# Gated mix of a long convolution and dilated local attention: transfers cut to multiples of 16 rows, the gate as a row, k and v all resident, late projections inside attention

## The chip, the cores and the metric

The kernel runs on one NeuronCore of a Trainium2 chip. TensorE (PE in the profile) multiplies matrices from SBUF into PSUM; VectorE (DVE) and ScalarE (ACT) move and change data between PSUM and SBUF; GpSimd (POOL) does small work and issues transfers; SyncE (SP) only issues transfers. All transfers, whoever issues them, run on 16 DMA engines. An engine works through its instructions in order, and so does the queue of a sequencer that issues transfers: an instruction that waits holds all behind it. The metric is the device time of one execution in microseconds.

## The reference

```python
g = sigmoid((x * gate_w).sum(-1, keepdims=True))      # x = A_q, [1, 2048, 640]
# branch a
k_shift = sum over t < 4 of shift_k[:, t] * k[s - t]  # causal, per channel
kv = k_shift * v
y = causal_convolution(kv, ssm_k) + kv * ssm_D        # by FFT over 4096 points
a = x * y
# branch b: 32 heads of 20 channels, window of 8 positions at a step of 2
q, k, v = split(x @ wqkv)
o = softmax(q[s] . k[s - 2 w] * 20 ** -0.5, w < 8, s - 2 w >= 0) @ v
b = o @ wo
out = g * a + (1 - g) * b
```

All inputs and the output are bf16.

## The kernel before

The program is written out by hand: instructions reach each engine in the order of the Python code, and a tile framework adds the waits. Memory is taken from pools; a pool that is closed leaves its room to later ones, whose first writers wait for the last users of what lay there. Of the transfers that SP issues, a new one waits for the one that was issued eight before it.

**Loading and v.** x is gathered into 18 tiles of 128 rows (`xS`): a tile holds two blocks of 64 keys, each with 57 queries and 7 rows before them, even and odd positions apart. `load_x` (L192) makes one transfer for blocks that are whole, and one of 57 or 62 rows where a sequence begins or ends. k is loaded as 16 consecutive positions in each partition, in four chunks of four, with a halo of three positions from the partition before (L216, 127 rows); v has two buffers (`vns`, L211), and chunks 2 and 3 are loaded from POOL's queue in `kv_gen` once a buffer is free. For each x tile PE makes five transposes (`transposes`, L280, evacuated by ACT to `xT`) and ten matmuls for v (`vproj`, L286, evacuated by ACT to `VW`).

**k*v** (`kv_gen`, L243) is DVE work: for each chunk four products with the taps (L248), two additions (L252, L255) and the product with v (L256) into a part of the same buffer `pr`, which POOL then writes to the scratch `kv_scr` (L260). It is advanced a step at a time between the PE work of the loops at L437 and L446.

**Gate** (`gate`, L301): 90 matmuls with one column each, exp, +1 and reciprocal, six transfers on POOL's queue that scatter the gate to `g_scr` in order of position (L314, L316), four that read it back (L318).

**q and k** (`qk_gen`, L331): five fifths (`ft`) of 128 channels; in each five groups of columns, k and q apart, five accumulating matmuls each (L340), evacuated (L342) to a staging tile `stg` with two buffers. When a fifth is done, SP sends its heads, 20 rows each, from `stg` to the attention's operand tiles `kq` (L355), where each head has 32 partitions: 20 channels and 11 feature rows that make the mask (`feats`, L323, eight loads of 374 KB). `kq[0]` lies where `xS` was, `kq[1]` where `kvw` (k and v) was; the latter's feature loads therefore wait for the last product of `kv_gen`.

**Attention**: 24 steps of four heads, in three groups `gi` of six x tiles each (eight steps `t` a group), each step in two halves. `scores` (L487) makes 24 small matmuls and one exponential into one of four `ET` buffers; `pv` (L501) makes 24 small matmuls into two PSUM tiles `O`, and after the second half DVE makes two reciprocals and two products. In the loop (L589) the scores of a half go ahead of the products of the half before. Beside it run `op_gen` (L573), the transposes and the output projection of the group before (one unit of work in a half, two in one of eight), and `ht_gen` (L469), 20 transposes on DVE of the filter `ssm_k`, which is loaded with its tap 0 corrected by `ssm_D` on POOL (`load_h`, L270). Results are stored to `b_scr` by two transfers of 57 rows per tile (`op_store`, L544). kv, G and wo are loaded as attention begins (L462 to L480).

**Convolution**: an FFT in matmul stages over five groups of 16 channels per quarter: `s1_gen` (L366) and `s2_gen` (L386) for the filter (h) and for kv (u); `h_s2` makes the copy `Hw` with its halves exchanged by two transfers (L406); `u_s2` multiplies spectra, four products on DVE after all four evacuations (L416, L417); `inv1` (L420) goes back. Evacuations go to ACT or DVE by a running estimate of their load (`Load`, L103). A last loop (L671) makes the last inverse stage, multiplies by the gated x (`qg`), adds the gated b (`bl`), and stores.

Of the kernel before, what the change touches and what calls it, by code (L numbers as in the profile page):

```python
# [131 lines left out]
def kernel(  # L132
# [33 lines left out]
    D5 = p0.tile([128, NG], BF, name="D5")  # L166
    gat = p0.tile([128, 18], F32, name="gat")
# [14 lines left out]
    wraw = pC.tile([128, D, 4], BF, name="wraw")  # L182
    wl = pC.tile([128, 4, D], BF, name="wl")
    pr = pC.tile([128, 4, 4 * D], BF, name="pr")
# [6 lines left out]

    def load_x(m0, m1):  # L192
        for sub in range(2):
            for m in range(m0, m1):
                k0, k1 = (PRE if sub == 0 and m % 9 == 0 else 0), (KB - 2 if sub == 1 and m % 9 == 8 else KB)
                if (k0, k1) != (0, KB):
                    nc.sync.dma_start(xs(m)[KB * sub + k0:KB * sub + k1],
                                      raw(x2, xrow(2 * m + sub, k0) * D, [[2 * D, k1 - k0], [1, D]]))
# [12 lines left out]
    vns = [kvw[:, (19 + 4 * e) * D:(23 + 4 * e) * D].rearrange("p (t d) -> p t d", d=D) for e in range(2)]  # L211

    def load_k(c):
# [3 lines left out]
        nc.sync.dma_start(kh[:, 3 + 4 * c:7 + 4 * c, :], raw(k2, 4 * c * D, [[16 * D, 128], [D, 4], [1, D]]))  # L217

    def load_v(c, eng):
        eng.dma_start(vns[c % 2], raw(v2, 4 * c * D, [[16 * D, 128], [D, 4], [1, D]]))  # L220
# [14 lines left out]
    for g in range(NG):  # L235
        nc.gpsimd.dma_start(D5[:, g:g + 1], raw(A_ssm_D, 16 * g, [[80, 8], [1, 16], [1, 1]]))
# [6 lines left out]
    def kv_gen():  # L243
        nc.vector.tensor_copy(wl[:], wraw[:].rearrange("p c j -> p j c"))
        yield
        for c in range(4):
            for j in (0, 1, 3, 2):
# [8 lines left out]
            nc.vector.tensor_tensor(pr[:, 2].rearrange("p (u n i) -> p n u i", u=8, n=4),  # L256
                                    pr[:, 0].rearrange("p (n u i) -> p n u i", n=4, u=8),
                                    vns[c % 2].rearrange("p n (u i) -> p n u i", u=8), ALU.mult)
            ld.t["d"] += 3000
            nc.gpsimd.dma_start(raw(kvs, 4 * c * 80, [[16 * 80, 128], [S * 80, 8], [1, 320]]),  # L260
                                pr[:, 2].rearrange("p (u m) -> p u m", u=8))
            if c < 2:
                load_v(c + 2, nc.gpsimd)
# [3 lines left out]

    hns = {}

    def load_h(g):  # L270
        hn = pA.tile([128, 2048], BF, name="hn", tag="hn", bufs=2)
        hns[g] = hn
        nc.sync.dma_start(hn[:], raw(A_ssm_k, IL * g * S, [[80 * S, 8], [S, IL], [1, S]]))
# [57 lines left out]
    def qk_gen():  # L331
        for ft in range(NDT):
# [13 lines left out]
            if ft == 0:  # L346
                feats(0)
# [374 lines left out]
```

## Time and profile before

| what | value |
|---|---|
| median of 2 runs | 417.5 us (417.04 to 417.96) |
| the profiled execution | 413.04 us, of which the span of the core is 410.6 us |
| mean granted TensorE clock of it | 0.728 |
| busy: PE, PEld (weight loads), DVE, ACT, POOL | 264.1, 190.4, 196.3, 175.2, 35.7 us |
| DMA | 48.95 MB in 15,152 packets, mean 119 GB/s |

The page cuts the span into 40 equal slices of 10.3 us; a digit is the busy share in tenths. The chain that ended last is followed back from the last instruction. A row such as "PE a L1 <- ACT b L2: 10, 3, 5" says that PE, at the instruction that writes a in line 1, waited three times for ACT, 10 us in all and 5 at most. A group's row gives the shapes, the count, busy us and mean ns, then the idle time before it. "issue" is time in which an engine waited for nothing that the profile shows.

### The profile page before, as it was taken

To read this page: it belongs to the slowest core of one execution; us is meant where nothing else is said; L and a number is where in the kernel's file an instruction comes from. 1 tells how busy PE (TensorE), PEld (TensorE's weight loads), DVE (VectorE), ACT (ScalarE), POOL (GpSimd) and SP (SyncE) were. 2 spreads that over 40 slices of the span, in tenths; PEclk is the share of its full clock that TensorE was granted. 3 is DMA by queue.
4 is the path that set the end of the run, shared out by engine and by line. 5 is a ranking of instruction groups with operands and counts; after the bars stand their busy time and mean duration, and the time that the engine had idled before them with its cause. 6 is when DMAs were issued, how large, how long until landed. Compare 5 with 4: busy or idle time off the path is not lost.

```text
span 410.6 us, 12313 instructions
## 1 busy us (share of the span) xinstructions
PE 264.1 (64%) x5611; PEld 190.4 (46%) x5616; DVE 196.3 (48%) x285; ACT 175.2 (43%) x292; POOL 35.7 (9%) x58
## 2 busy tenths in 40 slices
PE   1793099982965002773498999977644878678640
PEld 1572075540432000562365655655644867668530
DVE  0100689237015000392176833543752897966784
ACT  2483073513140002552243433432635696885372
POOL 6700011700110000000000000000000000000022
PEclk9998588996869555655555555799675798987875
DMA  7743877986523676469712010011599040429345
GB/s 205 158 125 103 271 276 114 110 174 90 136 72 62 86 128 129 99 165 211 282 51 81 18 32 24 28 42 58 124 213 245 17 105 4 105 54 232 80 106 155
DMA packets 15152, 48.95 MB, mean 119 GB/s; under 512 B 2639, under 2 KB 9661, under 8 KB 12700
## 3 DMA queue, kind: packets, MB, share of 16 engines
q1 hardware_dynamic: 12844, 42.11, 43.7%
q0 software_dynamic: 2256, 6.06, 6.7%
q8 instruction: 43, 0.70, 0.8%
q14 instruction: 9, 0.07, 0.1%
HBM read 29.43 MB, written 7.87 MB: 91 GB/s over the span
## 4 chain that ended last, share of the span: by engine, by line
DMA 27%; PE 26%; DVE 19%; issue 15%; POOL 5%; ACT 5%; SPq 1%; POOLq 0%; DVEq 0%; ACTq 0%
DMA kq<-stg 8%; DMA g_scr<-gat 6%; PE i L428 6%; PE op L553 6%; DMA Hw<-Hs 5%; PE O L521 3%; PE sc L496 3%; PE s L396 3%; DMA kv_scr<-pr 3%; DVE oS L531 2%; DVE hT L472 2%; DVE Hw L417 2%; DMA g_nat<-g_scr 2%; DMA b_scr<-fin 2%; PE tr L539 2%
## 5 line engine op out<-in xcount | busy, mean ns | idle before, releaser
L340 PE MATMUL pj<-xT,W 128*128 128x456 bf16 (+3 forms) x245 | 56.1, 395 | 47.5 <-ACT stg L119 47.2
L340 PEld LDWEIGHTS <-W 128*128 128x128 bf16 x250 | 27.0, 108 | 76.3 <-issue 57.8
L119 ACT CAST stg<-pj 128x512 bf16<-128x512 f32 (+3 forms) x50 | 24.9, 537 | 78.8 <-DMA kq<-stg 62.7
L499 ACT ACTIVATE ET<-sc 128x684 bf16<-128x684 f32 x48 | 35.4, 742 | 49.8 <-PE sc L496 48.5
L248 DVE TENSOR_TENSOR pr<-kvw,wl 128x2560 bf16<-128x2560 bf16 x16 | 23.1, 1483 | 68.8 <-DMA kv_scr<-pr 37.0
L472 DVE STREAM_TRANSPOSE hT<-hn 128x512 bf16<-128x512 bf16 x20 | 20.3, 1031 | 39.1 <-PE pj L340 39.1
L119 ACT CAST Am<-s 128x512 bf16<-128x512 f32 x59 | 31.2, 618 | 17.2 <-PE s L379 13.2
L428 PE MATMUL i<-M,Hs 128*128 128x128 bf16 x160 | 28.9, 269 | 9.1 <-DVE Hs L416 5.6
L553 PE MATMUL op<-wo,oT 128*128 128x320 bf16 x120 | 32.9, 432 | 2.8 <-DVE fin L558 2.6
L290 PE MATMUL psv<-W,xT 128*128 128x320 bf16 x180 | 30.3, 321 | 4.5 <-DMA W<-in_B_wqkv_dram 4.5
L428 PE MATMUL i<-M,Hw 128*128 128x128 bf16 x160 | 28.3, 268 | 4.3 <-DVE Hw L417 4.1
L396 PE MATMUL s<-Am,G 64*128 64x64 bf16 x1280 | 26.0, 203 | 7.6 <-DVE Am L121 3.9
L521 PE MATMUL O<-VW,ET 64*64 64x21 bf16 x1152 | 25.0, 203 | 8.9 <-issue 6.0
L496 PE MATMUL sc<-kq 31*64 31x57 bf16 x1152 | 25.0, 228 | 7.8 <-issue 6.1
L396 PEld LDWEIGHTS <-G 64*128 64x128 bf16 x1280 | 24.4, 104 | 9.1 <-issue 8.1
L496 PEld LDWEIGHTS <-kq 31*64 31x64 bf16 x1152 | 18.7, 141 | 19.6 <-issue 18.7
L428 PEld LDWEIGHTS <-Hw 128*128 128x128 bf16 x160 | 23.3, 156 | 8.4 <-DVE Hw L417 4.9
L428 PEld LDWEIGHTS <-Hs 128*128 128x128 bf16 x160 | 23.4, 157 | 7.4 <-DVE Hs L416 6.5
L521 PEld LDWEIGHTS <-ET 64*64 64x64 bf16 x1152 | 19.6, 142 | 12.7 <-issue 6.6
L529 DVE RECIPROCAL rd<-O 128x12 f32<-128x12 f32 x48 | 10.8, 224 | 28.5 <-PE O L521 28.2
L283 PE MATMUL trx<-ident,xS 128*128 128x128 bf16 x90 | 9.2, 244 | 23.2 <-DMA xS<-in_A_q_dram 23.2
L290 PEld LDWEIGHTS <-xT 128*128 128x128 bf16 x180 | 18.2, 105 | 11.6 <-issue 4.1
(65 smaller groups left out, 383.6 us busy)
## 6 DMA issues: line engine op xcount, KB each, us to landing
Hw<-Hs SPq DMA_DIRECT2D x10, 512.0 KB
kq<-stg SPq DMA_DIRECT2D x28, 170.2 KB
kq<-ca_feat SPq DMA_DIRECT2D x8, 374.3 KB
kvw<-in_A_k_dram SPq DMA_DIRECT2D x4, 640.0 KB
kv_scr<-pr POOLq DMA_DIRECT2D x4, 640.0 KB, 12.3
hn<-in_A_ssm_k_dram SPq DMA_DIRECT2D x5, 512.0 KB
kv<-kv_scr SPq DMA_DIRECT2D x4, 640.0 KB
qg<-in_A_q_dram SPq DMA_DIRECT2D x4, 640.0 KB
```

The source lines that it names most:

```text
L119: self.nc.scalar.copy(dst, src)
L248: nc.vector.tensor_tensor(pr[:, j].rearrange("p (n c) -> p n c", n=4), kh[:, 4 * c + 3 - j:4 * c + 7 - j, :], wl[:, j, :].unsqueeze(1).to_ ...
L290: nc.tensor.matmul(ps[:, 0:320], lhsT=xT[:, dt, 128 * m:128 * m + 128], rhs=W[:, dt, 2, n0:n0 + 320], start=(dt == 0), stop=(dt == NDT - 1))
L340: nc.tensor.matmul(ps[:, 0:nb * wd], lhsT=W[:, dt, which, 128 * ft:128 * ft + 128], rhs=rhs, start=(dt == 0), stop=(dt == NDT - 1))
L396: nc.tensor.matmul(o, lhsT=G[rows, j, r, :], rhs=Am[rows, 2 * j + r, :, :], start=(r == 0), stop=(r == 1), tile_position=(64 * c, 0), skip ...
L428: nc.tensor.matmul(o, lhsT=src[:, c, :, :, 8 * oc + il].rearrange("p q j -> p (q j)"), rhs=M[:, k, :], start=(k == 0), stop=(k == 1), skip ...
L472: nc.vector.transpose(hT[:, g].rearrange("p (c n) i -> p n c i", c=2)[:, 16 * p:16 * p + 16], hns[g][:].rearrange("p (a n) -> p n a", n=64 ...
L496: nc.tensor.matmul(sc[64 * sub:64 * sub + 64, hh, QB * mb:QB * mb + QB], lhsT=kqt[r:r + DH + NF, t % 4, si, 0:KB], rhs=kqt[r:r + DH + NF, ...
L499: nc.scalar.activation(ETs[i % NET][:, :, 0:NW], sc[:, :, 0:NW], ACT.Exp, scale=SCALE)
L521: nc.tensor.matmul(O_[s][64 * par:64 * par + 64, 21 * sl:21 * sl + 21], lhsT=ET[rows, hh, QB * mb:QB * mb + 64], rhs=VW[rows, NMB * gi + m ...
L529: nc.vector.reciprocal(rd[:], Ov[:, :, DH])
L553: nc.tensor.matmul(op[:, 0:320], lhsT=oTs[j][:, ft, :], rhs=wo[:, ft, 320 * hf:320 * hf + 320], start=(ft == 0), stop=(ft == NDT - 1))
```

## The change

Transfers. `load_x`, the halo and `op_store` are cut into a part with a multiple of 16 rows and a rest: 57 becomes 48 + 9, 62 becomes 48 + 14, 127 becomes 112 + 15. v has four buffers (`v23` is new), so that all of k and v is loaded on SP's queue, after all of x, and none on POOL's.

k*v. The product with v goes to its own tile `kvo` with two buffers; `kv_gen` is advanced from the first v tile on.

Gate. 30 matmuls with `wg` as the one stationary column give the gate as a row; six exps put it in order of position; SP writes it to `g_scr` in one transfer and reads it back in four; +1, reciprocal and 1 - g follow on DVE in `gate_end`.

Features. Only four transfers into the first of eight head slots; DVE copies the slot to the others, 14 copies.

q, k, v. k and q of a column group share one PSUM tile of two banks (three buffers), and likewise the two halves of a v tile, which ACT evacuates in one instruction. The last fifth of q/k and v tiles 12 to 17 are made inside the first attention group (`late_qk`, `late_v`), evacuated by DVE and ACT in turn.

Attention. The loop goes by whole steps: scores of the next step, then products, then late work, then two or three units of output projection. `O` is one PSUM tile of two banks with one buffer, with one reciprocal for both; the working PSUM tile `w` has two buffers instead of one.

Filter. No transposes: `load_h` makes eight transfers per group on POOL's queue, straight into the layout of the matmul (`h_lin`), in pieces of 64 elements; they, kv and G are issued when the first attention group is done. Tap 0 is corrected on DVE after attention.

Convolution. One evacuation for each s1 tile instead of two; the products with the spectra follow each of the four evacuations; the order of the s1 steps and the inverse steps changes.

```diff
+    def split16(n):
+        a = n - n % 16
+        return [(i, c) for i, c in ((0, a), (a, n - a)) if c]
...
-            nc.sync.dma_start(kh[1:128, 0:3, :], raw(k2, 13 * D, [[16 * D, 127], [D, 3], [1, D]]))
+            for p, n in ((1, 112), (113, 15)):
+                nc.sync.dma_start(kh[p:p + n, 0:3, :], raw(k2, (16 * p - 3) * D, [[16 * D, n], [D, 3], [1, D]]))
...
-    load_k(0); load_v(0, nc.sync)
     load_x(13, 18)
+    load_kv(0)
     load_w(1); load_w(0)
-    load_k(1); load_v(1, nc.sync); load_k(2); load_k(3)
+    for c in range(1, 4):
+        load_kv(c)
...
     def gate():
+        grow = pC.tile([1, S], F32, name="grow", tag="stg", bufs=2)
+        for c in range(6):
...
+                nc.tensor.matmul(gps[0:1, 0:6 * QB], lhsT=wg[:, dt:dt + 1], rhs=rhs,
...
+        nc.sync.dma_start(g_scr[:].unsqueeze(0), grow[:])
         for g in range(4):
+            nc.sync.dma_start(g_nat[32 * g:32 * g + 32, :], raw(g_scr[:], 16 * g, [[64, 32], [1, 16]]))
...
+        if e == 0:
+            nc.gpsimd.memset(kqt[:, 0], 0.0)
+            for h4 in range(4):
+                r = slice(32 * h4 + DH, 32 * h4 + DH + NF)
+                nc.sync.dma_start(kqt[r, 0].rearrange("p b c -> p (b c)"), ca["feat"].ap())
+    def feat_copies(e):
+        for t in range(4):
+            if e or t:
+                for p in range(2):
+                    ld.copy(kq[e][:, t, NSB * p:NSB * p + NSB], kq[0][:, 0, NSB * p:NSB * p + NSB], 800, eng="d")
...
+    def late_qk():
+        stg = new_stg()
+        for c in range(5):
+            for part in range(2):
+                ps = ppa.tile([128, 512], F32, name="pj2", tag="w", bufs=2)
+                qk_part(NDT - 1, c, part, ps)
+                qk_evac(stg, c, part, ps, eng="da"[part])
+                if (c, part) == (4, 1):
+                    qk_send(NDT - 1, stg)
+                yield
+    def late_v():
+        for m in range(12, 18):
+            for a in range(2):
+                ps = ppa.tile([128, 512], F32, name="pv2", tag="w", bufs=2)
+                vproj_half(m, a, ps[:, 0:320])
...
-    for m in range(18):
+    for m in range(12):
         vproj(m)
+        transposes(m + 2)
+        advance(kvg, 1)
+    for m in range(14, 18):
+        transposes(m)
     gate()
+    feats(0)
...
+    for k in range(20):
         advance(qk, 1)
         advance(kvg, 1)
+        if k >= 3:
+            advance(fc, 2)
+        if k == 12:
+            gate_end()
...
+    def load_h(g):
+        for q in range(4):
+            for c in range(2):
+                nc.gpsimd.dma_start(h_lin[32 * q:32 * q + 32, IL * g:IL * g + IL, c, :],
+                                  raw(A_ssm_k, (160 * q + 80 * c + IL * g) * S, [[64, 32], [S, IL], [1, 64]]))
...
+    for k in range(len(steps)):
+        if k + 1 < len(steps):
+            scores(2 * k + 2)
+            scores(2 * k + 3)
+        pv(2 * k)
+        pv(2 * k + 1)
+        gi, t = steps[k]
+        if gi == 0:
+            advance(lqk, (3, 3, 2, 2, 0, 0, 0, 0)[t])
+            advance(lv, (0, 0, 1, 2, 3, 3, 3, 0)[t])
+        if k == NT - 1:
+            sC.close()
...
+            load_h(0)
+            nc.sync.dma_start(G[:], cf["G"].ap().rearrange("p (a r b) -> p a r b", a=32, r=2))
...
+            for g in range(1, NG):
+                load_h(g)
         if opg is not None:
+            advance(opg, 3 if t % 2 else 2)
...
-        yield from s2_gen(("u", g), Up)
         Hs, Hw = st[("H", g)], st[("Hw", g)]
-        for c in range(2):
-            nc.vector.tensor_tensor(Hs[:, c], Up[:, c], Hs[:, c], ALU.mult)
-            nc.vector.tensor_tensor(Hw[:, c], Up[:, c], Hw[:, c], ALU.mult)
+        def prod(jb):
+            blk_ = lambda t_: t_[:, :, :, 8 * jb:8 * jb + 8, :].rearrange("p c q j l -> p (c q) (j l)")
+            for H_ in (Hs, Hw):
+                nc.vector.tensor_tensor(blk_(H_), blk_(Up), blk_(H_), ALU.mult)
+        yield from s2_gen(("u", g), Up, prod)
...
-                run("ababiabiabii", **gens)
+                run("ababababiiii", **gens)
```

More of the change, by code (lines that the diff above doesn't have):

```diff
@@ new lines, in qk_evac, with qk_send @@
+    def qk_evac(stg, c, part, ps, eng=None):
+        _, wd, _, z = QKP[part]
+        nb = 8 if c < 4 else 4
+        ld.copy(stg[:, 8 * c:8 * c + nb, z:z + wd], ps[:, 0:nb * wd].rearrange("p (b c) -> p b c", b=nb), nb * wd, eng=eng)
+    def qk_send(ft, stg):
+        for h in range(H):
+            r0, r1 = max(DH * h, 128 * ft), min(DH * h + DH, 128 * ft + 128)
+            if r0 < r1:
+                t, h4 = divmod(h, 4)
+                o = 32 * h4 + r0 - DH * h
+                nc.sync.dma_start(kq[t // 4][o:o + r1 - r0, t % 4, :, :], stg[r0 - 128 * ft:r1 - 128 * ft])
@@ L587 @@
     opg = None
+    lqk, lv = late_qk(), late_v()
+    steps = [(gi, t) for gi in range(NGI) for t in range(NT)]
     scores(0)
[L589 to L603 removed]
```

255 lines of the change are left out of this document (114 added, 141 removed).

## The prediction

> **What bounds the kernel now.** I read the page's parts 1, 2 and 4 first, then the waits, then the chain, then windows over the stages.
>
> ```profile
> span 410.6 us, 12313 instructions
> PE   1793099982965002773498999977644878678640
> DMA 27%; PE 26%; DVE 19%; issue 15%; POOL 5%; ACT 5%; SPq 1%; POOLq 0%; DVEq 0%; ACTq 0%
> ...
> PE trx L283 <- DMA xS<-in_A_q_dram: 23.2, 2, 16.2
> PE pj L340 <- ACT stg L119: 47.2, 3, 33.1
> ACT stg L119 <- DMA kq<-stg: 62.7, 3, 38.2
> DVE pr L248 <- DMA kv_scr<-pr: 37.0, 3, 20.9
> ```
>
> No engine is the bound as a whole: the largest share of the chain is DMA, and PE has holes in slices 4 to 16 (up to 167 us). The waits size them: one hole of 16.2 us in the transposes of x, and three holes, 47.2 us in all, where PE waits for ACT to empty a q/k accumulator, ACT itself waiting for the transfers out of `stg`.
>
> The first hole starts in SP's queue.
>
> ```profile
> 12.72 13.79 SPq L217 DMA_DIRECT2D kvw<-in_A_k_dram  x1
> ...
> 20.00:41.00 21.00, 14.14 (x128) 10.58 (x126) 0.00 (x0) 12.34 (x27) 0.00 (x0) 0.91 0.38 111
> 41.00:61.00 20.00, 10.67 (x80) 7.80 (x81) 15.80 (x10) 7.25 (x15) 1.46 (x2) 0.67 0.82 271
> ```
>
> In windows the last two columns are DMA share and GB/s. The load behind the 127-row halo of k holds SP for 13.79 us, and the DMA engines stand at 0.38 meanwhile: few of them do the work. The last x tiles queue behind it. After 41 us the same queue moves 271 GB/s.
>
> The other holes are one chain, here in order of time.
>
> ```profile
> 72.17 3.23 POOL g_scr L314 x2
> ...
> 79.10 26.59 DMA g_scr<-gat
> ...
> 116.91 4.23 DMA kv_scr<-pr
> ...
> 130.93 22.04 DMA kq<-stg
> 152.98 8.38 DMA kq<-stg
> ...
> kq<-ca_feat SPq DMA_DIRECT2D x8, 374.3 KB
> ```
>
> The gate's scatter (26.59 us) blocks POOL's queue, so the write of k*v chunk 2 leaves only at 116.91; DVE waits for `pr`, SP holds the second feature load until DVE is done, and the sends of the third fifth of q/k then share the engines with 4 x 374 KB of features (22.04 us), where the sends of a fifth alone take 8.38.
>
> ```profile
> 64.00:90.00 26.00, 25.84 (x131) 12.83 (x131) 11.94 (x9) 10.75 (x21) 8.93 (x8) 0.93 0.85 124
> 168.00:203.00 35.00, 18.14 (x841) 15.21 (x835) 16.45 (x40) 13.76 (x20) 0.26 (x4) 0.53 0.77 201
> 203.00:238.00 35.00, 32.31 (x769) 20.87 (x762) 24.38 (x51) 14.02 (x21) 0.57 (x3) 0.50 0.18 59
> 263.00:289.00 26.00, 19.86 (x392) 14.41 (x394) 11.99 (x28) 10.31 (x16) 0.00 (x0) 1.00 0.15 46
> ```
>
> Columns: window, length, busy time of PE, PEld, DVE, ACT, POOL, granted clock, DMA share, GB/s. Attention runs from about 167.5 to 289 us. Its middle third is PE-bound (32.31 of 35 us) at clock 0.50, though its end gets 1.00.
>
> **The change, part by part, as a new timetable.** The sum is made on the profiled span.
>
> *To the start of q/k (was 64 us).*
>
> ```profile
> 29.35 1.52 PE L290 MATMUL psv<-W,xT 128*128 128x320 bf16 x10
> L284 ACT COPY xT<-trx 128x640 bf16<-128x640 bf16 x18 | 12.4, 697 | 22.4 <-PE trx L283 22.2
> ...
> L305 PE MATMUL gps<-wg,xT 128*128 128x1 bf16 x90 | 2.4, 163 | 0.0
> ```
>
> Six of 18 v tiles leave: 6 x 1.52 = 9.1 us. The halo becomes 112 + 15 rows and goes behind all of x, so the 16.2 us hole goes; what is late next is nothing: 12 tiles last to about 32 us and x is some 4.4 MB with W and the filter, 16 us at 271 GB/s, 24 at two thirds of it. The gate becomes 30 matmuls of 342 columns, 0.16 us each by the row of 320 columns: 4.9 against 2.4 now, +2.5. Four trailing transposes go at ACT's 0.70 us: +1. So 64 - 9.1 - 16.2 + 2.5 + 1 = 42 us.
>
> *Four fifths of q/k (was 64 to 167.5).* 131 of 250 matmuls fill 26 us at clock 0.93, so a fifth is 9.9 us and four are 40: PE is done at 82. Sends keep pace (8.38 a fifth) with three accumulator pairs as slack. The features shrink from 8 loads of 374 KB to 4 of a quarter; the rest are 14 copies on DVE. The gate's 5 transfers move from POOL to SP: the sends now stand behind the landing of the gate's row, a few us, while the k*v writes stand behind nothing. The two PE holes before the third go; the third is replaced by DVE's k*v chain:
>
> ```profile
> L248 DVE TENSOR_TENSOR pr<-kvw,wl 128x2560 bf16<-128x2560 bf16 x16 | 23.1, 1483 | 68.8 <-DMA kv_scr<-pr 37.0 <-DMA kvw<-in_A_k_dram 31.7
> L252 DVE TENSOR_TENSOR pr<-pr 128x5120 bf16<-128x5120 bf16 x4 | 11.3, 2824 | 0.1
> L244 DVE COPY wl<-wraw 128x2560 bf16<-128x2560 bf16 x1 | 1.5, 1494 | 11.1 <-DMA wraw<-in_A_shift_k_dram 11.1
> kv_scr<-pr POOLq DMA_DIRECT2D x4, 640.0 KB, 12.3
> ```
>
> A chunk is 4 x 1.48 + 2.82 + two more of the first kind = 11.7 us, four are 47. Its first input lies 5.6 MB down the queue: 21 us at 271 GB/s, I take 25. Six feature copies come between, 2178 elements each: 1.27 us each by the copy row, 7.6 in all, and a wait of some 4 us for the features to land: 25 + 47 + 7.6 + 4 = 84. The first exponential's buffers lie where `kvo` lay, as far as the pools' order tells, so attention waits for the last k*v write: 4.2 to 12.3 us, I take 6. Attention starts at **90** (82 if PE alone counted, 97 at the upper prices). The Trainium skill, "VectorE: DVE Perf Modes", Rules for kernel authors, gives a dense bf16 copy in SBUF four elements a cycle, an estimate of 0.6 us each; then the six copies cost 3.8 and attention starts at 86. The only copy in the trace is strided, so no run here shows the dense one.
>
> *Attention, first group (was 167.5 to 203).*
>
> ```profile
> 225.15 0.65 PE tr L539 x5
> ...
> 226.70 1.45 PE op L553 x5
> 228.15 0.47 PE sc L496 x19
> 228.62 0.49 PE O L521 x21
> ...
> 264.19 0.84 PE L553 MATMUL op<-wo,oT 128*128 128x320 bf16 x5
> ...
> 264.96 0.38 PE L496 MATMUL sc<-kq 31*64 31x57 bf16 x24
> ```
>
> The upper rows are at clock 0.50, the lower at 1.00. A group's scores and products are 16 x 0.96 = 15.4 us slow, 12 fast (0.38 for each of the 32). The last fifth of q/k (9.9 fast, 19.8 slow) and a third of v (9.1, 18.2) come in. Fast: 31 us; slow: 53. These are long dense matmuls, like the 64 to 90 us window, so I take fast, with 6 us for a slow start and for the late sends, which the scores of t = 6 need: 37 us, to **127**. DVE's 20 transposes of h vanish, and its reciprocals halve in number; the single O buffer is covered by the late work and scores between two uses.
>
> *Second group (was 203 to 238).* The loads of kv and G move here from the first group, and with them its stalls:
>
> ```profile
> 191.07 0.48 PE L496 MATMUL sc<-kq 31*64 31x57 bf16 x18 [5.58 <-issue]
> 200.01 0.34 PE L521 MATMUL O<-VW,ET 64*64 64x21 bf16 x10 [5.96 <-issue]
> ```
>
> Both fall in the time when the queue moved 201 GB/s; PE waits for nothing that the profile shows. I take 9 of these 11.5 us, since the second group issues fewer instructions per us. Slow, the group is 12 x 1.45 + 6 x 0.65 + 15.4 = 36.7, which the 203 to 238 window confirms; fast it is 12 x 0.84 + 6 x 0.38 + 12 = 25 (a transpose taken as quick in proportion). Output projections now come two or three in a row instead of one between scores, so slow stretches should end sooner; I take 31 + 9 = 40, to **167**.
>
> *Third group and tail (was 238 to 289).* 25 fast, and for the last six tiles 6 x (2 x 0.84 + 0.38) = 12.4, 14 with waits for stores: 39, to **206**. Stores become 72 in place of 36, on an SP that has little else then.
>
> *Convolution (was 289 to 410.6, 122 us).*
>
> ```profile
> 298.02 19.11 DMA Hw<-Hs
> 349.78 1.23 DVE Hs L416
> ...
> 353.28 1.14 DVE Hw L417
> ```
>
> The copy Hw still queues behind 3.6 MB of qg and T (19.11). The four products (4.7 us, first and last of four rows shown) follow the last evacuation now; spread over it, about 1.3 stays. Over five groups they hold the chain for 12 us (if only the first two count) to 23.5; I take 15, so 9 are saved, less 3 because in the first group DVE now stops at its first product until Hw lands. Merged evacuations save perhaps 2. So 114, bounds 108 and 122. The additions of tap 0 are five tiny DVE operations.
>
> Sum: 90 + 37 + 40 + 39 + 114 = 320 span. The profiled execution took 413.04 for its span of 410.6, and the runs' median is 417.5, 1.1% above: 320 + 2.4 = 322, times 1.011 = **325**.
>
> **Rivals.** *Attention stays at half clock.* For it: 0.50 through 203 to 238 with PE 92% busy. Against: the denser blocks. It gives 53 + 46 + 37 + 15 = 151 in place of 116: 360 us.
>
> *The h loads gate the convolution, and the kernel gets slower.* The five loads of 512 KB become 40 on POOL's queue, 20,480 pieces of 128 bytes, from 127 us on; 79 us cover them, 3.9 ns a piece.
>
> ```profile
> L314 POOL DMA_DIRECT2D g_scr<-gat x4 | 6.4, 1596 | 0.6 <-DVE gat L309 0.6
> g_scr<-gat POOLq DMA_DIRECT2D x2, 2.0 KB, 26.0
> ```
>
> Issue alone at the L314 price (513 pieces) is 40 x 1.6 = 64 us, hidden. Landing: the k*v write moved 1,024 pieces in 4.23 us, 4.1 ns, 84 us in all: +5. The gate's 2,048 pieces of 4 bytes took from 72.2 to 105.7 us, 16.4 ns: 336 us in all, time 325 + 257 = 582. From about 8.4 ns a piece the kernel is slower than before. For the low price: the gate's scatter ran beside the sends of q/k in 57-row pieces. The Trainium skill, "DMA: Bandwidth & Descriptors", Specifications, asks for 512 bytes or more for line rate, which speaks against these loads; no run here shows 128-byte reads in bulk.
>
> *q/k stays transfer-bound*: sends of 20 rows are as before, and if the features or the gate's row land late each fifth costs 12 to 14 us instead of 9.9: 335 to 340. *The 16-row split does nothing*: then the 16.2 us hole stays in part, but halo after x leaves it to k alone: DVE's chain starts some 14 us later, 339.
>
> **How the numbers follow.** Main case 0.58 (300 to 345: attention from 82 to 97, groups fast or partly so, convolution 108 to 122); half clock throughout 0.20 (360); q/k or halo late 0.10 (335 to 345); h loads late but still a gain 0.07 (345 to 405); h loads slow enough to lose 0.05. Range 300 to 360, the likeliest alone 305 to 342. Two per cent is about what a measurement of this kernel can tell from no change: faster 0.93, same 0.02, slower 0.05.
>
> **What would show it.** Right: no wait of PE for x beyond 13 us; PE's waits for `stg` under 5 us; first exponential near 90, released by the last `kv_scr` write; clock near 1.0 in the first group; two stalls of about 5 us in the second; h landed before the last projections. Wrong: PE idle in the convolution's first stage until `h_lin` lands, clock 0.5 through attention, or ACT waiting for `kq<-stg` by tens of us.

## The result, and the profile after

The changed kernel takes 335.24 us (median of two runs, 332.93 and 337.55) where the kernel before takes 417.5: a ratio of 0.803, 95% interval 0.779 to 0.827. The forecast was 325 in a range of 300 to 360. Beside the runs further down the kernel before had medians of 404.6 to 414.1 us, so its 417.5 is on the long side and the ratio lies nearer 0.81 to 0.83. A run more than 1.5% above the fastest of its kernel counts as slow, and medians in this document are those of the other runs, while ranges take in all. The profiled execution took 337.55 us for a span of 335.7, so against the span of 320 in the forecast's sum 15.7 us are missing.

The page of the changed kernel, its span, PE's busy share and clock in 40 slices of 8.4 us, the instruction queue's share of DMA, and the chain by engine:

```profile
span 335.7 us, 12259 instructions
...
PE   1399899969549978643969987536696969677330
...
PEclk9999999999757997555877999567778797985855
...
q8 instruction: 43, 0.70, 0.9%
...
PE 35%; DVE 22%; DMA 13%; issue 12%; ACT 10%; SPq 5%; POOL 0%; DVEq 0%; ACTq 0%; POOLq 0%
```

From slice 3 to slice 10 (84 us), where the kernel before had its holes, PE is nearly full, and DMA has gone from 27% of the chain to 13%. The low digits are elsewhere: slices 11 and 12 (84 to 101 us), 17 to 19 (134 to 159) and most of what follows 208 us.

The same execution by stage: window, length, busy time of PE, PEld, DVE, ACT, POOL, granted clock, DMA share, GB/s. The last four rows are the three groups of attention, cut at the first exponential of each, and the convolution up to its first inverse matmul.

```profile
0.00:43.80 43.80, 29.95 (x240) 21.18 (x242) 16.85 (x11) 22.95 (x37) 16.27 (x22) 1.00 0.97 283
43.80:83.70 39.90, 37.06 (x200) 19.20 (x206) 31.72 (x24) 18.55 (x39) 2.85 (x3) 1.00 0.51 119
```

```profile
86.50:128.80 42.30, 33.23 (x827) 19.93 (x829) 19.05 (x43) 16.12 (x27) 2.05 (x5) 0.76 0.46 103
128.80:169.30 40.50, 26.28 (x870) 18.45 (x857) 13.06 (x34) 15.00 (x24) 24.53 (x39) 0.62 0.83 192
169.30:193.00 23.70, 20.20 (x810) 15.00 (x803) 12.28 (x33) 14.17 (x21) 1.24 (x2) 0.86 0.19 51
208.90:243.70 34.80, 18.86 (x544) 17.06 (x545) 19.95 (x24) 19.29 (x20) 0.00 (x0) 0.67 0.74 173
```

The same points in the two traces, the groups in both by their first exponentials:

| reached (us of the span) | before | forecast | after |
|---|---|---|---|
| start of q/k | 64 | 42 | 43.8 |
| PE done with the q/k made ahead | 167.6 | 82 | 83.7 |
| first exponential | 169.1 | 90 | 86.5 |
| start of the second group | 193.5 | 127 | 128.8 |
| start of the third group | 235.4 | 167 | 169.3 |
| start of the convolution | 286.9 | 206 | 208.9 |
| length of the convolution | 123.7 | 114 | 126.8 |

Up to the convolution the timetable held within 4 us at every point. The convolution was to gain 8 us and lost 3; with 126.8 in place of 114 it is 13 of the missing 15.7. Of the span 74.9 us are gained in all, and the table says where: 82.6 lie ahead of the first exponential. Attention takes 122.4 us where it took 117.8, now with a fifth of q/k and a third of v inside it, and the convolution 3.1 more.

What PE waits for now, first in the waits (total, times, longest), then in the timeline (start, length, the idle time before it in brackets):

```profile
PE s L445 <- issue: 11.6, 5, 6.7
PE sc L539 <- issue: 8.9, 3, 5.4
PE pj L349 <- ACT stg L119: 7.7, 2, 5.0
PE O L561 <- issue: 4.9, 1, 4.9
```

```profile
98.50 2.29 PE L349 MATMUL pj<-xT,W 128*128 128x512 bf16 x5 [5.00 <-ACT stg L119]
...
135.98 0.55 PE L539 MATMUL sc<-kq 31*64 31x57 bf16 x26 [1.69 <-issue]
146.56 0.33 PE L539 MATMUL sc<-kq 31*64 31x57 bf16 x9 [5.43 <-issue]
155.50 0.66 PE L561 MATMUL O<-VW,ET 64*64 64x21 bf16 x35 [4.90 <-issue]
172.82 0.37 PE L539 MATMUL sc<-kq 31*64 31x57 bf16 x10 [1.76 <-issue]
223.36 0.88 PE L445 MATMUL s<-Am,G 64*128 64x64 bf16 x26 [6.73 <-issue]
```

The three holes of 47.2 us in q/k are down to 7.7. The largest sum is now "issue", time in which PE waited for nothing that the profile shows: 12.0 us in the second group (1.69, 5.43 and 4.90), 1.76 at the start of the third, 6.73 in the first stage of the convolution. Those of the second group and of the convolution fall where DMA is full (shares 0.83 and 0.74).

### The profile page after: what moved, and what is told of

The parts are those of the page before. It is cut to its first block, busy times and chain, and to the rows that moved or that the text cites. A ratio compares the mean times of both kernels' runs of the same rounds, so it can differ in the third digit from the quotient of the medians.

```text
span 335.7 us, 12259 instructions
## 1 busy us (share of the span) xinstructions
PE 238.3 (71%) x5549; PEld 175.0 (52%) x5556; DVE 188.4 (56%) x279; ACT 168.8 (50%) x247; POOL 52.9 (16%) x81
## 4 chain that ended last, share of the span: by engine, by line
PE 35%; DVE 22%; DMA 13%; issue 12%; ACT 10%; SPq 5%; POOL 0%; DVEq 0%; ACTq 0%; POOLq 0%
PE i L482 8%; PE op L595 6%; DVE pr L256 6%; PE s L445 5%; DMA kq<-stg 5%; ACT Am L119 4%; PE O L561 3%; DVE pr L260 3%; PE sc L539 3%; DMA xS<-in_A_q_dram 3%; PE pj L349 3%; DMA kvw<-in_A_k_dram 3%; DVE kq L121 3%; SPq L363 2%; ACT Up L119 2%
## 5 line engine op out<-in xcount | busy, mean ns | idle before, releaser
L119 ACT CAST stg<-pj 128x456 bf16<-128x456 f32 (+3 forms) x45 | 21.4, 531 | 35.0 <-PE pj L349 17.7
L445 PE MATMUL s<-Am,G 64*128 64x64 bf16 x1280 | 25.6, 201 | 15.9 <-issue 11.6
L631 POOL DMA_DIRECT2D h_lin<-in_A_ssm_k_dram x40 | 25.8, 650 | 56.0 <-PE sc L539 40.3
L445 PEld LDWEIGHTS <-G 64*128 64x128 bf16 x1280 | 23.7, 103 | 17.4 <-issue 15.6
L119 ACT CAST Am<-s 128x1024 bf16<-128x1024 f32 x25 | 24.1, 1060 | 12.8 <-PE s L430 8.4
L755 POOL DMA_DIRECT2D out_dram<-qg x12 | 6.0, 502 | 154.6 <-DVE qg L753 154.6
L595 PE MATMUL op<-wo,oT 128*128 128x320 bf16 x120 | 25.4, 359 | 3.8 <-ACT oT L582 2.3
L539 PE MATMUL sc<-kq 31*64 31x57 bf16 x1152 | 16.9, 206 | 14.6 <-issue 8.9
L568 DVE RECIPROCAL rd<-O 128x24 f32<-128x24 f32 x24 | 7.4, 306 | 34.5 <-PE O L561 34.5
L287 PE MATMUL psv<-W,xT 128*128 128x320 bf16 x120 | 20.8, 326 | 5.1 <-DMA W<-in_B_wqkv_dram 5.1
L119 ACT CAST Cm<-i 128x1024 bf16<-128x1024 f32 x13 | 13.1, 1012 | 19.7 <-PE i L482 19.7
L582 ACT COPY oT<-tr 128x640 bf16<-128x640 bf16 x18 | 12.5, 692 | 20.0 <-PE tr L579 19.7
```

The source lines that it names most:

```text
L119: self.nc.scalar.copy(dst, src)
L287: nc.tensor.matmul(ps, lhsT=xT[:, dt, 128 * m:128 * m + 128], rhs=W[:, dt, 2, 320 * a:320 * a + 320], start=(dt == 0), stop=(dt == NDT - 1))
L445: nc.tensor.matmul(o, lhsT=G[rows, j, r, :], rhs=Am[rows, 2 * j + r, :, :], start=(r == 0), stop=(r == 1), tile_position=(64 * c, 0), skip ...
L539: nc.tensor.matmul(sc[64 * sub:64 * sub + 64, hh, QB * mb:QB * mb + QB], lhsT=kqt[r:r + DH + NF, t % 4, si, 0:KB], rhs=kqt[r:r + DH + NF, ...
L582: nc.scalar.copy(oT[:], tr[:])
L595: nc.tensor.matmul(op[:, 0:320], lhsT=oTs[j][:, ft, :], rhs=wo[:, ft, 320 * hf:320 * hf + 320], start=(ft == 0), stop=(ft == NDT - 1))
```

## The experiments

All edits are made to the changed kernel. Where two runs are compared, the lengths of stages from their traces are used beside the times. The times of one kernel spread over 1 to 3%, so 2 or 3 us can't be read from them alone.

### The parts that made the gain: rows of 16, and the gate

```diff
-        return [(i, c) for i, c in ((0, a), (a, n - a)) if c]
+        return [(0, n)]
...
-            for p, n in ((1, 112), (113, 15)):
+            for p, n in ((1, 127),):
```

The loads of x and the stores to `b_scr` go whole here as well.

> The changed kernel with the multiples of 16 rows taken back: loads of x with 57 or 62 rows, the halo of k with 127 rows and the stores to b_scr with 57 rows go whole again; the places in the queues stay as they are. Theory G (the split is what counts; the forecast's rival gave 339 us for a split without effect): the halo holds SP for about 14 us, DVE's k*v chain ends about 14 us later, the stores of the tail land in 3.6 to 3.9 us instead of 1.4, in all 12 to 25 us slower. Rival H (the place behind x did it alone): within 4 us.

Measured: 360.78 us (359.69 to 361.48), ratio 0.8815 (0.875 to 0.888). Three rows of its timeline and the window of the first, then the same window of the changed kernel:

```profile
19.42 13.67 SPq L225 DMA_DIRECT2D kvw<-in_A_k_dram  x1
...
50.34 5.70 DVE L256 TENSOR_TENSOR pr<-kvw,wl 128x2560 bf16<-128x2560 bf16 x4 [36.72 <-DMA kvw<-in_A_k_dram]
...
54.49 27.15 PE L349 MATMUL pj<-xT,W 128*128 128x512 bf16 x127 [11.59 <-DMA W<-in_B_wqkv_dram]
```

```profile
19.40:33.10 13.70, 13.70 (x127) 10.49 (x125) 0.00 (x0) 10.90 (x18) 0.00 (x0) 1.00 0.25 59
```

```profile
19.40:33.10 13.70, 13.70 (x129) 10.57 (x128) 4.79 (x4) 10.75 (x17) 0.00 (x0) 1.00 1.06 300
```

PE does the same work in both windows, but DMA moves 59 GB/s in place of 300, because SP stands behind the halo of 127 rows. With the halo behind x, what comes late is W for q/k (11.6 us of PE) and the first input of the k*v chain: its first product starts at 50.34 us and not at 28.30. So the chain is 22 us late, where theory G had 14; the first exponential comes at 107.3, 20.8 us later, and from the last exponential to the convolution, where the stores lie, it takes 2.9 us more. Theory G holds, at the top of its 12 to 25. The Trainium skill, "DMA: Bandwidth & Descriptors", Why a DMA increments its semaphore by 16 and not by 1, says that a transfer is spread over the largest number of engines up to 16 that divides the slowest dimension on both sides, and names 127 partitions as a case with one engine. The trace's list of DMA packets agrees: the 127 packets of the halo, 3,840 bytes each, go one behind the other there, from 26.6 to 48.2 us and never more than two at once; in the changed kernel up to 16 of them run at once, from 21.0 to 25.9 us.

For the gate its old functions were put back: 90 one-column matmuls, six scatters and four loads on POOL.

```diff
-        nc.sync.dma_start(g_scr[:].unsqueeze(0), grow[:])
...
+                nc.gpsimd.dma_start(raw(gs, 2 * QB * sub + e, [[2, QB], [4 * QB, n], [1, 1]]),
+                                    gat[KB * sub + PRE:KB * sub + KB, 9 * e:9 * e + n].unsqueeze(2))
...
+            nc.gpsimd.dma_start(g_nat[32 * g:32 * g + 32, :], raw(gs, 16 * g, [[64, 32], [1, 16]]))
```

> The changed kernel with the old gate: 90 matmuls of one column, and six scatter transfers and four loads on POOL's queue in front of the writes of k*v, with the second buffer of kvo kept. Theory I (the gate on POOL's queue was the cause of the third hole): the write of chunk 1 or 2 leaves only when the scatter has landed, some 26 to 34 us after the gate; DVE stands at kvo, the k*v chain ends 8 to 15 us after 86.4 and the time grows by as much, less 2.5 us of PE. Rival J (two kvo buffers hide it): within 3 us.

Measured: 357.94 us (357.67 to 361.29), ratio 0.8766 (0.868 to 0.885), 22 us above the changed kernel's 336.05 in the control run below. From its timeline:

```profile
63.53 2.04 POOL L321 DMA_DIRECT2D g_nat<-g_scr  x4 [6.12 <-DMA g_scr<-gat]
...
67.42 3.73 POOL L333 MEMSET kq<- 128x4356 bf16 x1 [0.15 <-issue]
...
78.62 1.37 DVE L121 COPY kq<-kq 128x2178 bf16<-128x2178 bf16 x2 [21.78 <-DMA kq<-ca_feat]
...
92.32 2.93 PE L353 MATMUL pj<-xT,W 128*128 128x512 bf16 x7 [22.71 <-ACT stg L119]
```

POOL's queue is the cause, as the forecast said, but what stands behind the scatter is not a write of k*v: it is the memset of the feature slot. The features land late, DVE waits 21.78 us for them at a copy, the k*v chain behind the copy waits with it, and PE stops for 22.71. Theory I had the place right, the victim and the size (8 to 15) wrong.

These two parts are 25 and 22 us of the gain. That features now come in four loads and copies instead of eight loads, and that k, v and `kvo` have more buffers, was taken back in no run; what these are worth is not known.

### Late projections inside attention

```diff
-        for ft in range(NDT - 1):
+        for ft in range(NDT):
...
-    for m in range(12):
+    for m in range(18):
...
-            advance(lqk, (3, 3, 2, 2, 0, 0, 0, 0)[t])
-            advance(lv, (0, 0, 1, 2, 3, 3, 3, 0)[t])
```

> The changed kernel with all q/k and v products made before attention again (18 v tiles, five fifths), nothing late inside the first group. In the control on its chip the first exponential came at 86.6 us and the first one of the second group at 128.0. Theory K (moving the products only filled a wait; their 19 us of PE work are the same at either place): the first exponential comes at 102 to 105 us, since the last fifth now covers the wait for the third fifth's sends, the first group takes 15 to 18 us in place of 41.4, the second group begins at 118 to 122, and the time falls by 5 to 9 us. Rival L (the long matmuls inside the first group keep the clock high and cover the waits of scores, exponentials and products for each other): without them the first group has a clock near 0.5 and takes 22 to 28 us, the second begins at 126 to 131, and the time is within 3 us of the changed kernel or up to 3 us longer.

Measured: 342.0 us (338.91 to 343.34), ratio 0.8298 (0.822 to 0.838), which still touches the interval of the changed kernel. First exponential at 105.8, near theory K's 102 to 105, but the first group then took 39.1 us:

```profile
105.80:144.90 39.10, 12.78 (x744) 10.83 (x743) 6.70 (x20) 11.14 (x18) 11.64 (x18) 0.56 0.93 196
```

```profile
112.92 0.81 SPq L656 DMA_DIRECT2D G<-cf_G  x1
...
122.29 0.71 PE L538 MATMUL sc<-kq 31*64 31x57 bf16 x47 [5.43 <-issue]
133.38 0.43 PE L538 MATMUL sc<-kq 31*64 31x57 bf16 x16 [8.72 <-issue]
143.69 0.62 PE L560 MATMUL O<-VW,ET 64*64 64x21 bf16 x32 [7.56 <-issue]
149.62 0.72 PE L538 MATMUL sc<-kq 31*64 31x57 bf16 x48 [3.32 <-issue]
```

PE is busy 12.78 of 39.1 us. The clock of 0.56 is what L expected, but the time goes to three stalls, 21.7 us in all (5.43, 8.72 and 7.56; the last row's 3.32 lies in the second group). xT and W give up their room earlier, so G, kv and h are loaded from 112.9 us on, straight into a group that has only small matmuls. Both theories fail on the main point: K had 15 to 18 us for the group, L 22 to 28. By these rows the late work buys, above all, that the loads start behind the first group.

### What the stalls without a cause are

In one experiment G and kv alone were issued one by one, each behind a store of the second group; in the other h as well, over the second and the third:

```diff
+            if pending:
+                nc.sync.dma_start(*pending.pop(0))
```

> The changed kernel with the five loads of G and kv not issued at once behind the first attention group but one at a time (G in two halves), each behind a store of a finished tile in the second group. Theory B (big loads in a row starve PE of its instructions, because each 16 KB packet of the instruction queue stands behind them): the stalls without a named cause in the second group, 13.8 us in all (1.7, 5.4, 4.9 and 1.8), shrink below 4 us, and the time falls by 8 to 12 us. Rival D (the 40 loads of h in pieces of 128 bytes cause them, or the program itself): the stalls stay within 3 us of 13.8 and the time within 3 us. If G or kv land too late, PE waits for them in the convolution's first stage.

```diff
+            pending += [0, gl(0), 1, gl(1), 2, kl(0), kl(1), 3, kl(2), kl(3), 4]
...
+                    nc.gpsimd.tensor_copy(tick[:], fins[j][0:1, 0:1])
+                    load_h(nxt)
```

> The changed kernel with the loads of h, G and kv issued one group at a time (0.5 to 1 MB each), each behind a store of a finished tile in the second and third attention groups: the eight transfers of an h group wait on POOL for one element of the tile just finished. Theory B' (whatever keeps the engines full holds up PE's instructions, the h pieces among it, since spreading kv and G alone left 10.6 of 13.8 us): stalls without a named cause under 4 us in the second group, which ends some 10 us earlier, and 8 to 12 us off the time. Rival M (the program stalls there whatever is loaded, or the paced loads stall PE in the third group instead): within 3 us of the changed kernel beside it.

> The changed kernel as it is, as the control on this chip for the runs beside it and for the ones before: 331 to 337 us, ratio 0.80 to 0.82; its convolution, 127.2 us in the first profile and 123.7 to 128.5 in the five runs that left its code alone, again within 123 and 129.

| kernel | median us (range) | second group | third group | start of convolution |
|---|---|---|---|---|
| changed | 335.24 (332.93 to 337.55) | 40.5 | 23.7 | 208.9 |
| changed again, f0 | 336.05 (335.14 to 338.60) | 41.1 | 24.3 | 211.4 |
| d1, G and kv spread | 335.77 (332.94 to 338.07) | 33.9 | 28.4 | 207.4 |
| f1, h too | 330.94 (329.35 to 338.13) | 30.5 | 30.4 | 206.8 |

```profile
128.40:158.90 30.50, 24.60 (x868) 17.47 (x858) 13.35 (x35) 14.79 (x24) 13.13 (x23) 0.72 0.36 98
158.90:189.30 30.40, 22.73 (x806) 16.42 (x800) 12.09 (x32) 14.27 (x22) 8.99 (x17) 0.72 0.73 162
```

These are the second and third group of f1. With the DMA share of the second down from 0.83 to 0.36, the group loses 10 us, as B' said; the third, which now gets the loads (0.73 in place of 0.19), takes 6 to 7 us more, as M said. Of the stalls over 1 us, the second group keeps 4.2 us of 12.0 and the third has 6.1 in place of 1.8. So each theory is right about one of the groups: a good part of the cost goes where the loads go. The two groups together take 60.9 us instead of 64.2 (65.4 in f0). The median is 5 us below f0's, but the ranges overlap, and over all runs it is 2; neither the 8 to 12 of B' nor M's limit of 3 is shown by the times. d1 lies between: stalls of 1.2, 3.0 and 3.8 us in its second group and of 3.8 in its third, the second 6.6 us shorter, the third 4.7 longer, the time unchanged. Its theory B had the time wrong, its rival D the second group.

The mechanism shows in the trace's list of DMA packets. The queue "q8 instruction" moved 43 packets, 16 KB each. Each long stall ends a short and nearly equal time after such a packet began:

```
changed kernel: packet begins  133.44 144.00 152.72 169.96 220.59 231.37
                PE goes on     135.98 146.56 155.50 172.82 223.36 234.12
f2:             packet begins  119.89 130.63 140.96 146.75
                PE goes on     122.29 133.38 143.69 149.62
```

That is 2.4 to 2.9 us in ten of ten. In all fourteen traces 103 waits of PE over 1.5 us have no named cause; each ends 2.2 to 3.5 us after a packet began. And PE goes on at even steps of its program: counted in all the instructions of PE in the trace (matmuls, weight loads, semaphore waits), the ends of the first three long stalls of the changed kernel lie 256 apart, and from one of the 103 to the next of the same trace it is always a multiple of 256, to within 2. So PE goes on when its next piece of program has come, and the piece waits behind the loads. That the stalls follow the loads was shown by f1 and f2; how the two queues share an engine was not. Loads are not the only ground: in the last loop of the convolution, whose matmuls are short (148 in 1.48 us), the changed kernel has a stall of 2.27 us while the DMA share is 0.02.

### The hole at 92 to 98 us

```diff
-            advance(lqk, (3, 3, 2, 2, 0, 0, 0, 0)[t])
-            advance(lv, (0, 0, 1, 2, 3, 3, 3, 0)[t])
+            advance(lqk, (0, 3, 4, 3, 0, 0, 0, 0)[t])
+            advance(lv, (4, 1, 0, 0, 2, 3, 2, 0)[t])
```

> The changed kernel with the late v products first and the last fifth of q/k a step later (calls per step 0,3,4,3 and 4,1,0,0,2,3,2 in place of 3,3,2,2 and 0,0,1,2,3,3,3). Theory E (PE stands from 92.4 to 98.5 us because the staging tile of the last fifth waits for the sends of the third, and other work is at hand): the hole shrinks to under 2 us and the time falls by 4 to 6 us. Rival F (the last sends come later by as much, and the scores of t = 6 wait for them): the hole moves to t = 6 or 7, time within 2 us.

Measured: 335.13 us (334.1 to 337.08). The hole of 5.0 us is down to 1.81 and 0.63:

```profile
93.65 2.82 PE L287 MATMUL pv<-W,xT 128*128 128x320 bf16 x10 [1.81 <-DVE VW L121]
...
114.78 0.38 PE L539 MATMUL sc<-kq 31*64 31x57 bf16 x23 [1.17 <-DMA kq<-stg]
117.43 0.38 PE L539 MATMUL sc<-kq 31*64 31x57 bf16 x23 [1.14 <-DMA kq<-stg]
123.69 0.38 PE L539 MATMUL sc<-kq 31*64 31x57 bf16 x23 [1.41 <-DMA kq<-stg]
```

Short waits for the last sends come in its place (3.7 us in these three, 4.6 with one of 0.92; the changed kernel has 1.9), and the second group begins at 127.9 instead of 128.8: theory F.

### The convolution

```diff
-        yield from s2_gen(("u", g), Up, prod)
+        yield from s2_gen(("u", g), Up)
+        for c in range(2):
+            nc.vector.tensor_tensor(Hs[:, c], Up[:, c], Hs[:, c], ALU.mult)
+            nc.vector.tensor_tensor(Hw[:, c], Up[:, c], Hw[:, c], ALU.mult)
```

> The changed kernel, with one part of its convolution put back: the spectral products follow all four evacuations of a group (four instructions of 2048 elements in place of eight of 1024 spread over the evacuations). The convolution took 127.2 us where the forecast had 114. Theory A (the new order costs): the first products stand in DVE's queue until Hw lands, so undoing them brings the first inverse matmul nearer to the landing and the time falls by 3 to 6 us. Theory B (the loads of qg and T cost: PE stands 6.7 us without a named cause and Hw lands 24.8 us after the start of the stage): no change, within 2 us. Theory C (the forecast's own term: spread products save 9 us, and the loss lies elsewhere): slower by 6 to 12 us.

```diff
-                run("ababababiiii", **gens)
+                run("ababiabiabii", **gens)
...
-                run("bbbbiiii", **gens)
+                run("bbibibii", **gens)
```

> The changed kernel, with the old order of first-stage and inverse steps in the convolution (two first-stage steps, then an inverse step, and so on, in place of all eight first-stage steps ahead of the four inverse ones). Theory A: the inverse matmuls no longer wait behind the merged evacuations on ACT, which the chain shows in rows of 4.7 and 4.8 us in two groups: faster by 4 to 8 us. Theory B: within 2 us. Theory C: the spread products need the evacuations to come first, because the inverse stage waits for the last product: slower by 2 to 6 us.

The third has both, and `ld.copy` of 512 elements twice in place of 1024 once in `s1_gen`:

> The changed kernel with all three edits of the convolution put back (products last, old interleave, two evacuations for each first-stage tile); the filter stays as it is loaded now. Theory A: the convolution comes to 114 to 119 us, the time falls by 8 to 13. Theory B: within 3 us of the changed kernel, the stall of 6 to 7 us in the first stage and the landing of Hw some 25 us after its start stay. Theory C: slower by 9 us or more, 136 us of convolution.

In the fourth the loads of qg and T stand behind `run("abababab", a=h_s2(0), ...)` instead of ahead of it:

> The changed kernel with the five loads of qg and T issued behind the first Hw transfers instead of ahead of them. Theory B: PE's stall of 6.7 us in the first stage goes or shrinks below 2, Hw lands 10 to 14 us after the start of the convolution instead of 24.8, and the time falls by 8 to 12 us. Theory A: Hw lands earlier, but what follows (evacuations on ACT, products on DVE) was the limit anyway: faster by at most 3 us. If the stall stays while no load of qg is under way, neither is right about it and it belongs to the program itself.

| kernel | median us (range) | convolution | to the first inverse matmul | the rest |
|---|---|---|---|---|
| changed | 335.24 (332.93 to 337.55) | 126.8 | 34.8 | 92.0 |
| changed again, f0 | 336.05 (335.14 to 338.60) | 125.4 | 35.6 | 89.8 |
| c1 products last | 331.38 (330.12 to 333.35) | 120.2 | 31.4 | 88.8 |
| c2 old interleave | 330.69 (328.99 to 333.48) | 119.0 | 29.7 | 89.3 |
| c3 all three old | 334.40 (332.08 to 337.43) | 126.3 | 29.7 | 96.5 |
| c4 qg, T later | 331.69 (331.02 to 340.27) | 126.7 | 31.3 | 95.4 |

The ratios of c1 to c4 (0.802, 0.800, 0.808, 0.804) are too near each other for the times to decide. The stage is clearer: in the eight profiles that leave it alone (the changed kernel twice, d1, d2, f1, f2, a1, a2) it takes 123.7 to 128.5, 125.8 in the mean; c1 lies 5.6 below this mean and c2 6.8, both below all eight. So, taken one at a time, each of the two edits costs the changed kernel some 6 us, as theory A said, and C, the forecast's own term, falls for this kernel. But c3, which undoes both, gains nothing in the stage: what follows its first inverse matmul is 5 to 8 us longer. Two rows of its page:

```profile
L486 PE MATMUL i<-M,Hs 128*128 128x128 bf16 x160 | 27.2, 258 | 10.4 <-DVE Hs L474 6.6
L486 PE MATMUL i<-M,Hw 128*128 128x128 bf16 x160 | 26.3, 256 | 4.2 <-DVE Hw L475 4.2
```

The inverse matmuls wait 10.8 us for products there, where they wait 4.7 in the changed kernel, 5.3 in c1 and 6.7 in c2; the stalls without a cause behind the first inverse matmul are 9.9 us there and 8.5, 8.5 and 9.2 in these three, so they explain little of it. The two edits depend on each other: with the inverse steps late, products last are better (c1 against the changed kernel); with the inverse steps mixed in, the waits for products speak for spread ones (c2 is 7.3 us shorter than c3 in the stage, 3.7 in the median). How much of that is the divided evacuation, which c3 has and c2 has not, stays open. (In c2 and c3 the first inverse matmul also comes earlier by the order itself. The profiles of c3 and c4 are of their longest runs, 337.43 and 340.27 us, and their last columns are long for that.)

For c4 B is half right, and the median is some 4 us below the changed kernel's, where B had 8 to 12. These are the first product of the changed kernel, which DVE holds until Hw lands, and that of c4 with its stalls:

```profile
233.29 0.69 DVE L469 TENSOR_TENSOR Hs<-Up,Hs 128x1024 bf16<-128x1024 bf16 x1 [3.17 <-DMA Hw<-Hs]
```

```profile
228.38 0.69 DVE L469 TENSOR_TENSOR Hs<-Up,Hs 128x1024 bf16<-128x1024 bf16 x1 [2.79 <-DMA Hw<-Hs]
...
232.52 2.00 PE L445 MATMUL s<-Am,G 64*128 64x64 bf16 x68 [5.83 <-issue]
```

Counted from the start of the stage, Hw lands after 16.6 us instead of 24.4. The stall of 6.73 did not go; it moved behind the loads (5.83 here, and 3.82 at 242.6).

### A version that beats both

The paced loads of f1, the late v first of d2, the interleave of c2, and qg and T spread over the first three Hw:

> The paced loads together with three more edits: the late v products ahead of the last fifth of q/k, the old interleave of the convolution, and the loads of qg and T spread (two of qg behind the first Hw, two behind the second, T behind the third). If the gains add (8 to 12 for the paced loads, 2 for the late v, 4 to 7 for the interleave, 4 to 8 for qg and T by theory B), 310 us; if the convolution is held by evacuations and products and only rearranged by these, 318 to 325; if the loads do not matter, 328 or more.

Measured: 318.80 us (317.23 to 325.67) beside 336.05 (335.14 to 338.60) for the changed kernel on the same chip; the ranges don't overlap, and the medians stand as 0.949 to 1. In the profiles, of f3's longest run and of f0's, attention from the first exponential to the convolution takes 121.0 us instead of 124.8, and the convolution 117.5 instead of 125.4. Its first inverse matmul comes 22.5 us after its start, not 35.6. The gains don't add to the full 310: two thirds of the 26 us arrive, within the 318 to 325 of a convolution that is only rearranged.

## Why the forecast was right, and where it was wrong

The total lies in the range because the timetable up to the convolution held, and that in part by luck: errors of the k*v chain, the first group and the second cancel, as shown below. Of the signs named ahead, three came (no wait for x, two stalls of about 5 us in the second group, h landed in time). Three did not: PE's waits for `stg` are 7.7 us and not under 5, the first exponential is not released by the last write of k*v, and the clock of the first group is 0.76 and not near 1.0.

**To the start of q/k**: right (42, measured 43.8), and a1 shows the term behind it. Its size for a split without effect, 339, was too small: 361.

**q/k**: right (82, measured 83.7), with the gate off POOL as its cause (a2). The forecast named the k*v writes as the ones that the scatter held up; in the new order it would be the features.

**k*v and the start of attention**: the chain ended at 86.4 (forecast 84), by errors that cancel. Its first product came at 28.3, not 25, and it waited 7.9 us for sends, not 4 for features; the copies were mis-sized the other way: 5.62 us for eight, 0.70 each, where 1.27 was taken from the strided copy. The estimate from the Trainium skill, "VectorE: DVE Perf Modes", Rules for kernel authors, 0.6, was nearer; the trace agrees with it to 0.1.

```profile
66.47 1.37 DVE L121 COPY kq<-kq 128x2178 bf16<-128x2178 bf16 x2 [7.91 <-DMA kq<-stg]
...
84.92 1.49 DVE L265 TENSOR_TENSOR kvo<-pr,v 128x2560 bf16<-128x2560 bf16 x1
...
86.51 2.75 ACT L542 ACTIVATE ET<-sc 128x684 bf16<-128x684 f32 x4 [2.13 <-DVE g_nat L319]
...
86.91 5.62 DVE L121 COPY kq<-kq 128x2178 bf16<-128x2178 bf16 x8
...
97.91 0.54 ACT L119 CAST stg<-pj 128x456 bf16<-128x456 f32 x1 [8.65 <-DMA kq<-stg]
```

The step "attention waits for the last k*v write" was wrong: the first exponential follows the last product by 0.1 us. What was late next had not been named: the eight copies stand before the sends of the third fifth, and the last fifth waits for its staging tile. (The bracket of the exponential names an older DVE instruction; the product ends at 86.41.) The first group still ended within 2 us of the forecast, since it started 3.5 us early and took 5.3 us more than its 37.

**First group**: its end was right (127, measured 128.8), its length was not (37, measured 42.3): 5.0 us went to the staging tile, and the clock was 0.76 where the sum took full clock. Half clock throughout, the rival at 0.20, falls: 0.76 in the first group, 0.86 in the third. The windows that the forecast called the first and second group before, 167.5 to 203 and 203 to 238, were cut by eye; by the first exponentials these groups took 24.4 and 41.9 us. The terms were added up from rows, so the sum does not hang on the cuts.

**Second group**: 40 against 40.5, by two errors that cancel. The stalls were 12.0, not 9; the rest took 28.5, not 31.

**Third group and tail**: right, 39 against 39.6 (23.7 us to the last exponential, 15.9 behind it).

**Filter loads**: landed in time, as the main case had it, though f1 beside d1 shows that they take part in the stalls. The list of transfers, and POOL's first and last rows of them:

```profile
h_lin<-in_A_ssm_k_dram POOLq DMA_DIRECT2D x40, 64.0 KB, 4.0
```

```profile
129.08 5.15 POOL L631 DMA_DIRECT2D h_lin<-in_A_ssm_k_dram  x8 [40.32 <-PE sc L539]
...
158.37 12.17 POOL L631 DMA_DIRECT2D h_lin<-in_A_ssm_k_dram  x19 [0.18 <-issue]
```

The median one lands after 4.0 us, and the last lands at 173.2, 36 us before the convolution. The 512 bytes for line rate of the Trainium skill, "DMA: Bandwidth & Descriptors", Specifications, which were weighed against them, did not decide here: all 20,480 pieces went in some 44 us, 2.2 ns a piece.

**Convolution**: the step that failed is "spread over it, about 1.3 stays" and with it "so 9 are saved". c1 shows that in the changed kernel the spread products cost some 6 us. The saving itself was not empty: with the old order of steps (c2 against c3) spread products and merged evacuations together gain 7.3 us of the stage, in one profile each, near the forecast's 9 - 3 + 2. It was counted for an order that the change gave up. The forecast looked at DVE's sum of work and not at what stands behind the first products in DVE's queue (3.17 us for Hw, and the evacuations of the next stage behind that). The other step is an edit that had no term at all, the order of the steps, which costs some 6 us beside spread products (c2). In the chain of the changed kernel ACT makes five evacuations in a row before the inverse matmuls can start, in two groups,

```profile
255.76 4.72 ACT Am L119 x5
...
273.46 4.80 ACT Am L119 x5
```

and no such row stands in the chain of c2. The two costs can't be added: taken off together they would leave 113 us, and c3, which divides the evacuations as well, has 126.3.

## What to carry to other kernels

Cut a transfer so that its rows divide by 16 before moving it in the queue: the halo held up whatever stood behind it, x in one order and W in the other. Ask of every operation that is moved forward on an engine what then stands behind it, and count the order of steps as an edit with its own price, which can turn the price of the edit beside it round. Where PE stops without a cause while DMA is full, pace the loads, but look where they go: a load moved out of one stage can stall the next.

## What the runs showed of the hardware

PE's program itself comes by DMA, 16 KB or 256 instructions at a time, and waits behind bulk loads. With a DMA share of 0.83 to 0.93 and small matmuls this cost 12.0 us in one group and 21.7 in another, in stalls of up to 8.7 us. Over all traces such stalls end 2.2 to 3.5 us after an instruction packet began, multiples of 256 instructions apart.

One halo of 127 rows, 488 KB, cut the DMA share to 0.25 for 13.7 us, its packets one behind the other; cut into 112 and 15 rows, with up to 16 packets at once, it left the share near 1.
